# A planned kernel of attention and gated FFN layers: another task order, other planned landing times, fewer zero-tile matmuls at the start

## The chip, the cores and the metric

The kernel runs on one core of one Trainium2 chip. Its time is the device time of one execution in microseconds (us); the median of several runs is compared. A separate profiled execution gives the trace and the profile page.

## What is computed

Four layers follow each other on x (2048 positions of 512 values): recurrent attention, FFN, attention, FFN, the same weights for both pairs. Each adds its result to its input and works on the layer norm of its input.

```python
# attention, 32 heads of 128; 64 segments of 32 positions, with 8 memory rows
for s in range(n_seg):
    h = jnp.concatenate([mem, xs], axis=1)            # 8 + 32 rows
    q, k, v = h @ Wq, h @ Wk, h @ Wv                  # per head
    p = softmax(where(mask, q k^T * scale, -1e9))
    o = (p v) @ Wo
    mem = o[:, :M]; outs.append(o[:, M:])
# FFN: (sigmoid(x @ w_gate) * (x @ w_up)) @ w_down,   512 -> 1792 -> 512
```

The memory makes segment s + 1 wait for segment s, so attention is a chain of 64 steps. Everything is in bf16 with sums in f32.

## The kernel before

**Tiling and stages.** Both attention layers run in one loop of 70 steps (`emit_step`): step t works on segment t of the first layer and segment t - 6 of the second, side by side as 80 columns. In steps 0 to 5 only the first layer has a segment, in steps 64 to 69 only the second: these are the thin steps, with 40 columns. A step takes the heads in six groups. For each group: projections q and k (line 892), a copy out of PSUM on ScalarE (ACT), scores (906), softmax on VectorE (DVE) with the exponential on ACT (920 to 937), transposes of the probabilities (949), a copy that spreads them (`spread`, from line 954), their product with the values (975), a copy, and the product with Wo (993). The end of a step copies the new memory rows into the next step's input `hT` (1006, 1011) and the output rows into `oxT`.

Values come in another way. `v_pass` and `v_half` (695, 732) project whole blocks of positions ahead of time and write them through DMAs to a scratch in DRAM (`scr`); each step reads its slices back into `vsb` (line 861, issued on SyncE, SP). Rows that depend on the memory are projected inside the step, as a strip of 32 columns for all heads (`strips`, 817), and go from `sst` to `vsb` by DMA (line 872, SP). A block of 128 positions (4 steps) that is finished goes through the FFN (`ffn`: transposes 1063, gate and up 1095, down 1119); its weights don't stay in SBUF, so that each of the blocks loads them again by transfers of 256 KB that GpSimd (POOL) issues (1087, 1088, 1113). At the start SP issues all attention weights (`load_weights`, 591), about 16 MB, in a fixed order of arrival, while TensorE (PE) works on values of the first blocks.

**What sets the order.** Nothing is issued where the code stands. Every operation is added to a list of 13,280 tasks (`Planner.add`, 214) with its engines, a planned duration, a latency `lat` until others may use its result, the keys that it reads and writes, and bytes for a DMA. `plan` (251) unpacks `SEQUENCE`, a compressed list that gives each task a rank, and `forward` (272) plays the program through in planned time: whenever an engine is free, it takes the ready task with the lowest rank that its buffers allow. For the kernel before, the ranks in `SEQUENCE` are the order in which the tasks start in that plan. The resulting order is the program: each engine executes its tasks in it, and waits on semaphores where data aren't there yet. So the planned times don't reach the chip; the order does, and so do three things that are drawn from the planned times:

- which of ACT and DVE takes a copy that either could do;
- the pace of the FFN weight loads: each waits on the chip for the PE task that ended just before its planned start (`add_manual_dep`, line 1240), so that POOL, which executes in order, is held by PE;
- zero-tile matmuls: where the plan leaves PE idle for over 250 ns, `warm` (415) puts matmuls of an all-zero tile `hot` ahead of the next task, in pieces of 128 columns, four to an instruction (line 1218). They write to the bank that the next task overwrites.

For transfers the plan keeps a bus time (`bus`, 372) for all DMAs together; a DMA is done at the later of the bus and of the end of its issue plus `lat`. `lat` is 4300 ns for a slice from the scratch (863) and 3200 for a strip (874). SP may have eight transfers under way in the plan (378 to 380).

Of the kernel before, what the change touches and what calls it, by code (L numbers as in the profile page):

```python
# [20 lines left out]
P = 128  # L21
MEM = 8
SEG = 32
L = MEM + SEG
LW = 2 * L
XS = 24
# [27 lines left out]
;Ag)rXk7pcfB%7A@!gH@5PER9zwFwU*Txh6(FIfkX|(7J?i&Gymhh!kX3<9*It9&+^ANuZ3nQF%vjb@k;)ADNDw~7A&yK6rftjYT<(0_Cu$F5_QL}_k&+#M$g4fMAuI3%VR%9II^4edG>hLecVFKKZ  # L54
fiq<zaDy4oUFv58J8W8}M`2{oi5UUb^!f*Ro0Ll?vc4MO@r^c`&wF^g&x{e8(wi=&1jnm{X}@GBNB?B98ftnN@q;Urg_TN7gRljNIZ1xL04!;{jd2yH$?cL&EwR4Y4Tqu8pK|P3tu<gW{h$`ab{UE_
fqK5_Bs&J*b^6-QBtiB1Rm-Zu8Nlc!2f&|gEyzQ&Zou|%s7^3{5zh9KTUR}tya8Oc6!P`{0)Vq8I;Cl`Bjt~AjrB%)CqD@z82Z2w;QrC0`{pXpx_R2Wh&&#2H3QIv3WnP|a@1!GQgacw;pKW^M`R|!
Nk+QQ;DjyYF5GF7!M*<sd8cVD>2uHyj70Z$6aD8lSDtqSMB#M+!9iZef2n{|jXj7clA2G^EzqM!g-lB)@}v+s<dLTg#Kii~);*dJP_OtPjOrD`dCRS`B*?af^G#|5&z)YMf)|%^UO;YbIwUZ94H|;|
&I8kZBVH%Vr|M`z4VQLMuW2mhCo%WGrCP@C3|aBQ!Z@sF?{dn1nHiX-Hcv2SE;6gPREA8v1gxUN5fjwov7s7E=){nUleMkl)rSwf-#NWnt+iLb)vYQSg8NO|ck6a&f5J`jCYy?w$`JBYrP7VoA#kkX
>yw8_VzTSGOpj8yq?_x;;hBH;rz~q4SdF9ZBg{rG@)htW>FtF!fG!q1a8hR)S^e6}q?Lzs^}+^#ob7fH!>Fyt6Ec%(XxD2g=*h~t0x*|HYIgpYBcJ&io_?o{l)`4GU_@%j@)8o~)(WjyR`I-_DVdEX
qpsq`mM61>+(8TaM-5>9Drz=jnb)-=yYKy|4I>K@zHNw@rcCC|=f*ye&WaMflMV5|xPNyTb*H)NgH9?jw1M*`|Aqy&^a*rUk;3mH)kGJznF1RvY3@t@=2^xaH0-f1Ty6gB5>G7cN@NTPLrchUmPhHP  # L60
BPzZ2ia}YU1q5^?Zh`JV^|-uLP^j5y#P_ZT06?ozV2jLQSp96AT@omT@9`T$m-yy@g4kD5^7&#?)KvIhz5<IDDn_B}S$w_%O54$*Uf&%*f!G9A0k)w2S80jRm_OzzD}%&|JCO=Jux2;jsV1&&*ocDe
vv19OW<}n=z=BXtevuQth?wJcFw3v~A;KU0Fj8U7v;-ubd1)6$LvOp^(EF2YN4lWzA>9UsIioM@psu~u&Horxi#{K)nGF~9<5jCnBT^6l!UsB(k4o)!8A~I>f8#r%yu%<R0mYyTfZ<)Sni2UT(vn0#
tm2cI5k@+Ojklj8V{nBRX$UB+gfBzr^hrH>$u5kX5;NqVjvk?&E^!9Un709~&!yGdZ`zS12GJ~~o>$PW0_Q(~(ech%@Dd4F?a@?s&4w?B3X^B#o>$WuxPHlU8E1h;6sRCPM;Cb&M89tcFI3Fc7SaL-
@ko8IZK`J@W2GEGmX}g(7vDTBKpV{0l0Fa*zKW5nQtSNYScG9m-W4oihEpRM9oZhx$s8@o43g~=;)6hTN^z^Shvggyiw$J(S&trHsZko5QCciufS!$?n=$+iEW_#~(`j}&V4WCWgYlK!d#Qs8!?9zj
+bqOxo_kt*eZ7rE@04&B0z8Nz9i<d40QttTz6^4LDi~8yhg8P4NzvULMSQJ-$b!TRs-7IAd_l8GT;#XHgZcX$-$b)HgDh{d9p!Ey5NK#kZ(Nzsu&svhey17&ct5)NozyL<4jW>hTpOmDH`UV?uNeKn
ulL27>(f<<fI2lD7P@{ZxKK5izxo4o_!^ec%pEaQr`~plAyRxTVWrISSzr8X5TfH(1GV1AzqFJC@ZL5V(+q2z_(&=mUZDhaes!D&m_4JvmfF?Tb1D<p2^ZH$QTP$`?ht%YJSK>L&CcqNEJ<!Kr{4oz
vj+K3Emf<Ch%)`ULp{|Z!2<pl7r@(XMSkbViiH_g;!i$l%ewSb&20V3maX%pZQ9=^qZ9wc+A{sGfKnIIgZi9N`Aj$1&p0a=tUVPau*9x6O+3z+=cQwW#v2L`O$oZv0t|=^q0+3wovlZqw;CjluSfY1
7;)b2dM;AEItw!IJo9aZVFG>~c1D!+Q8oJ6gHCVjgh+q=g5RV7n;S4Z{Vb-#GBbB5;S`h<JtFjk*+%dBbL|0-RP<JoBUp$?mRdco7QSmHHji-UX7~{&TCk0xhlix|OcNZzn$a?dwXxy6toswR3nCxg
<$l)jDf(|Z9;2QA2Pa?Sr*59(v?!>Gw*!qSrriD#k;zlQ3O)3BertDQxc3{@%R7C#_YLB_AsNpEq&sbpzKmH~RYP~bk{Zd_?;Wo1EPM{r9g$C}>3;0X_dxzhSf2(<dWtt@E+CAb_+p>QbPZxM{{PS3
*en5KD&!3JofsA3^5fe+Yc=aOqR)fM<|mNjpQ}L_L`b6F5Z9!0Ny_KiYa1f=>UfHv5NT}Dt#)}&@tB}*TmVzJN!1wQ308W#%Ewt9=zute@fBG_bJI~rE8@x(8H9zT)JiPkVik)hOISJpJ`Z|aqfuxS  # L70
9MY^{ThVokOpd=UmpouWZAyJ+>Q&s<TSe0J7BeE=BIr=gLszKqR~2v6Y6>hu2k+cm^UC_1#1b|?t!P7;XyfV~lp@ZnPb$}EWnWzg)_Pm2Q2jbtP7fuO#3di=k)6Dpo<n|F!K`{GgUY<TL&xEiPlsLE
&`&N90i`ZrB`F!^X2xQ#Z*X7g10f8gpm<n@MdGTPU@}*SmWq{(s7(9g_Cv(?{N1{2oaF^jfe$o_VK4qMF^xSK*{cee3e$;(u_$eW`lc&g&EI&y4i*uW%6zw-NX1hb(pOJBbt)zq^a*_i4QZU3OsA`a
ogk8T2n3iX4#2Ol?c4h;A1AqM9wA^Jr*lL?l6X!W4a}idB0|TS{P^F0xoo=H?n}?x#S)J57?AP`%qwl>;dln_?FWE@z$Yf>Vqz`|dwyR1uaTh&cJ&l`kd!X_?-X)Uh(;|b$81Dn>eA?1v=O~yq6@bR
lvtg%>-}E)I4o%t7|qUp0K%C@$IO_3Q8c<f2sy?3NQKPEsTbru3QRD|F$a4d@f{&HJW`|O6+dZE$zQ(5B{Er!7rj;f4B;-AE4MX{;f6HfmZJze6(XM=l9u^A_U!OD95{V?ww{=>wQP72Z~s4Qm*vR?
e*y&gf*;_)**=M^LbI7dC46mRe<kfr+>_l^QZ>lm(OXgC(MLi@qI+N!-8i=oU4&L8DE2q;wf%=IK%<}jzPwj}l6xHHB!-gZcv^HoZ{V!;w_?ExVSCPsDrsA{#Sb51#5b-20&?c^99>Nt=R8W4MSi*l
MCgAULe{=wE<IiLPE}6f&Z9CBTjxxm#$_7R6;Z-ebVg&LO>WXD!Pep6L3A0rMfMW?E%7v;VO`&f|Ap|wZ??;v^Q~wr_4FD&tZm<<vV<O6&>j+yJH$*U-MCo}`YUh|$58?UEU%S|;`YMe5WJlSWE_kL
E)LRM0MQ6r<a(5C^kO>B<W_mrR)FViX&=9@G;RSwumdZ&Qt1(0oIO6ak`3nRTF(wTL^pIe!t#dYVm=<rx<3Qr+huU{k!&q2AKPMS@{}fFPJPOl#O~xT)AjxxLZv|mhvohJ9z}-?!-FGN&=ldq)4r!D
*cp!V%Xw+RfahwLc)Ig{IHF)!SEG<NE#(9Yjhv#WJHTKEisY~5+qr=eRZhP)FaoF64N_9o35pnE(v8PoEVgW0r7x!jM^tenC7jjy!)MB3AcYWC48j5cMuv^}G6mD{UWyge2qtcY@;VQVZW$|axO~Oh
vJ(=-Q@Ew*P=dF|XXgO7`vJ<K48cKaSn5!FbYSw;t|wilbDVKhl?<VuNKghUS_lENW9>r$n!HW<BYwx!DFqn}AM7hQA@+s#m*u9N`b@Ma9m(V@dcecx`>pXpHMrdvT!$c6$7K*gPb#>jO6SUnwQF@S
>&t@I)gR?aZ}gYOy@|#4pu_GanAT5qv_jCS5Bv&znUe*1UBapE&|l`w?O1MdgnZ0R>Mw-E2=S@|2~OEKN1d=5kb0C<kwu$H!>xGujj568I8SGM7M8A~PmPpMktJ_zpry#uUGFxUxwuGjCr~0sf2+7g  # L80
1QQD+ok!zeEc-N#r4j85HjD_IIP7)bE0pBeVVwgpGLUF`aXcEYnas+nct*2CTatDY-UO860yp_D;wWRpnHqVob|AJG7Eu_;>7MspwFG-#th34g)A=(1$WWqkU;dyO*fYj89O$tHXy+9?G6n&!nE-bT
uHD2FL;P#J3)5yM(sJ4mXzUH7K%MW7ut6#aKE_VEm8Zy-<yJf7`JD;Ds5Y`Z;5r^JhiwaiY`Yzu+r<wjQ5Jo3qztp-Yaeftih>wiGv?Z>PImvDU$@!v+b{k6>d0r$Nyk>FDKbk@R8n3?EwnO2Jg_HM
^&{BYQ8~-q2UvBMkkT}=lF||tq88|}HA%Z!Mt#`v=86No_G8L~#*ll=e=mHZvdY}~2W}KZX>Q6&iLKNDoZhI7TM(m#F!*Py7hpHcsLyRcn)4c;_seEgk97w&NXraXv<}|Yrx`T)jmEs3KDJqcrl)v+
a`E{XIOU{=9wyfA_Qe6Fg7PICy+z0rWItXRiR_fcrE1b+YtfpKgby_i#DiZ#q>GE6gKJTEca-j*m_AZaS4r+{5`fIsD&Eka>#T$1h%?;0L<5{vRMqk<8KPEk@Hw2d(cY(lH4`Vc4`a4Z=uhAXua01S
d}N%2@j4-Sn=puE>7zRCBiN}PtDL0phD3sq=I<r8HJ|%r%nhYL7_BikjSVR7+}$I#^phFzOtMlRr9wvktyrcN>^S>5uX~y;KOZ)07B|Qpvfzi}nE<fV`fY&4nmh5Vo=gj<YM<Et2XL=k(Gfy+aAziY
!^T6yS=iPENu&kYb=FMz$XP>`DbpK9ox{*OWEvuP-dmBN%G*ZNlp2hSa77%g8H}Q_vPe%^C_Wp@)l$iHJrqj#=?~-%OjTBz7-kBg`I(xH^>eR@G<Em|wx>|WJt-xLE^W6up^P9~Kzun|byk~JEL#qF
UT%u3pg>u~N>iFXr84s{rky2t>t)1^hbyS|duHgv<R>(*@EcY|68IFb_x<JivX6sMv3lk=G4)l-D|&A(+awSm>pxhC=g<Ailb*)61+`*VtE_9f)yaAZnZx0`&xUz9Bi)0ndpC81IL=Fj>o}=}Ch^mD
a{YD<DQ#UfTxfqfn^-c6BC>YaC?R{qp)yf?p^3FV`^;lp-G8kVmKY3DqUL^S7g8+yJY4Vqq+(;q2YardKTJIIfSm;hAPuL(^{=YS2(t@2CS#O|s>c+=cuo2pLjY8Q$x#DV6Zej6Z6+s2Jao_#6eB^N
7a5P*6g-Zs{MHJT@<NVSs+drmT7C3uX>~(ur1;DdnN#UDYL?v7!!Fre<D_&r)ysX~u$jJpBXkHfi3^CbRQiN2#eVj4*Y&1Y9&Yd62}WPCU&?}1jk)^<;Xj%lk#*xH0J&?acOayDsi(r9Pg2arChoLZ
-c0{UkOgOWe7F;kG@*`6JA3Tn`bJM{0HY}ewITRwN+$1#PQS@f-e0GvY)0$_E>?k<uwxEv0N7%EmpAT;Pguj6d{Vby55>>*K-;Iy`XUw~a}xZd?9AV_f!CW0v1lx`Y@Mez3s_!eUd;`Q1*q_s7(F>=  # L90
4|BDtOk7rIPYp}7tPpCvbDyozSV)N#SL-t8I#V*{;CN%gQSVpsRe{_W<u{-?#aIGWPKK%H>**?-Ee>E?+#s+xtjt>}|33G7$N>I7i12j!u*RF%AAMnT$i@ZE-;Dgde8ZKEW37GCDnvi=le%JSa+G{n
+&Iei>EHmn=Fsxv|3C+uBlYDwTeYMZ&|8yf!>xC<lEgQzP+}DO)!F0Rf-DyHJ&<4G8eX2f+_P;6p&iv_V7UBs;C9F-9w+M|V%Dl{fMndP&kvo}d~iFsz7en-le9_u7*050e=zT3TWENVzx4zpe*EaN
E_R$wJ-6^dPSSK@HOiCva7<DlXkg9$A4q~qoev;f>xEG5`j|;}P6atT6JKHMeOBIUD!T7j@4=|Nf2Mg|DNFxWR&Hobs33JvVoFWbB(+u~7S$IxLqhyuGE&<vvl{CyO&z1oqHfh|2xyX5WdT^mjU{tL
qaiR6CykR9^~7dzlRAX3MnyC%)N&8XzzBT>bv5sR!f20Ha(j*RX9WbB&PIxchc5h=Fmjcqzgq1c{LF1WAx56-)nRxBt(DTxU^e<pf5p<J$)x~lc3BEtc>5LooO%n>XFGs~e{wNRGFTg$-_-?oHq5=9
w4PjSRCtdm*_=uiYlvVz!YpcU&k&0W4`R>fm7lQteSFF!M_52KaD|hF4CV}>6@KAW_}6k%yr)uH5D+@!u!nR>=?c#?EH^}0gd<j=cI~S7NNJIjZ-;~~8~e*@$)xkTbtoPX8<ePoaKkwZfMKsxKmi0a
GuEMV*kIW9?cN!r2{Z}sRkM}Hp5K)F0tm@-G^~vb{o~t{NOIx4)$8Ga?v>%CZ73bbqe-h(VGLXgCktybTz0o?*E>l{R4ioO9icVr#Jc5)aU&C~A(1}LPak#aaOk$ttY*Q>Q>`CmI4~tQH4Rm@q>AcG
?R9df05%CgU-Pl14SM+nGMMPk&7`&ID>$|s48-otrEtg9kZZs)L+Zk9Nq1c>2IhbA`rKc1L|lOdv395d@BqQ!ZW)c&jT3=)jt-4AomSOAN>}-+7UgX$PQR8kPkU=(C_~M3H8RWgDI*wT6%5ZSNsgs^
@`+tryad9d!c$`q7#<gIBN`WEv|-=;q=6=-NNKI5N(Z+cjzi^+wN~=rb_XnLICCEjg{eVEW=&t+zXa@WrA38tA1)DC&=s`b`b6z{%beoMIYj(s$g%D*K;Hz;p&*5f%6hl7ZLwiUm$bqc=)TbL>Z(9z
# [55 lines left out]
class Task:  # L154
    __slots__ = ("eng", "dur", "lat", "fn", "deps", "succ", "tail", "boost", "ndep", "ready", "start", "idx", "on", "fresh", "acq", "rel", "durs", "tick", "prev", "land", "adj", "banks", "rate", "nb", "after")

    def __init__(self, eng, dur, lat, fn, boost):
# [6 lines left out]
        self.adj = {}  # L164
        self.banks = ()
        self.rate = 0.95
        self.nb = 0
        self.after = None


# [19 lines left out]
class Planner:  # L190
# [9 lines left out]
    SPAN, COLD, WARM0 = 3413.0, 8000.0, 1200.0  # L200
# [1097 lines left out]
```

## Time and profile before

| | |
|---|---|
| median of 3 runs | 1785.14 us (1785.05 to 1786.47) |
| span of the profiled execution | 1781.3 us |
| instructions | 91,977 |
| matmuls recorded | 39,873, of them 109 of the zero tile |
| DMA traffic | 270.66 MB, mean 152 GB/s |
| granted TensorE clock | 1.000 |

The span runs from the first to the last instruction of one profiled execution; the runs of the table's first row are timed apart from it and 3.8 us longer. In the profile PE stands for matmuls and PEld for weight loads, which overlap them; ends of matmuls are modelled, and a few of the 512-column records are missing. SPq and POOLq are the queues that issue DMAs. A row of a timeline gives start, duration, engine, line, operation, output and input names, how many instructions were merged, and in brackets the idle time of the engine before it and what ended it. `L1232` and `L1234` are the helper lines through which all copies go.

### The profile page before, as it was taken

The numbers are of one execution on the slowest core, as the hardware profiler recorded it, in microseconds if no ns is written. First come the engines' busy times: TensorE is split into PE (matmuls) and PEld (weight loads), VectorE is DVE, ScalarE is ACT, GpSimd is POOL, SyncE is SP. The second block draws the span as 40 slices with busy tenths as digits, with TensorE's granted clock in tenths as the row PEclk, the third lists the DMA queues.
The fourth block names the chain that finished last, engine by engine and source line by source line (L and its number), as shares of the span: only waits on it lengthen the run. The fifth ranks groups of instructions, "written<-read, shape, count | busy, mean of one in ns | idle before, by whom it ended". The sixth has DMA issues, their size and how long they took to land.

```text
span 1781.3 us, 91977 instructions
## 1 busy us (share of the span) xinstructions
PE 1754.0 (98%) x39873; PEld 1517.1 (85%) x40083; DVE 1144.1 (64%) x3931; ACT 1167.8 (66%) x2973; POOL 573.8 (32%) x828
## 2 busy tenths in 40 slices
PE   9999999999999999999999999999999999999998
PEld 4688888888888898989898898988888888989886
DVE  4376666776577666756666676657656665666675
ACT  6676666666666666666766666666666766667564
POOL 5314031513233242323324241333324232333332
PEclk9999999999999999999999999999999999999999
DMA  9825254635555464445546453555555454555543
GB/s 342 265 74 165 59 155 121 195 105 158 146 162 153 133 174 136 139 137 165 160 130 198 135 161 106 154 160 167 156 148 172 111 145 140 158 156 139 165 143 94
DMA packets 131943, 270.66 MB, mean 152 GB/s; under 512 B 30394, under 2 KB 65090, under 8 KB 131538
## 3 DMA queue, kind: packets, MB, share of 16 engines
q0 software_dynamic: 56240, 181.91, 34.7%
q1 hardware_dynamic: 75298, 82.86, 16.3%
q8 instruction: 314, 5.14, 1.3%
q14 instruction: 91, 0.75, 0.1%
HBM read 220.41 MB, written 25.69 MB: 138 GB/s over the span
## 4 chain that ended last, share of the span: by engine, by line
PE 91%; DVE 5%; ACT 2%; issue 1%; DMA 1%; SPq 1%; POOL 0%; ACTq 0%; DVEq 0%; POOLq 0%
PE bank L892 31%; PE bank L993 17%; PE bank L1095 11%; PE bank L695 8%; PE bank L817 7%; PE bank L975 4%; PE bank L906 4%; PE bank L1119 4%; PE bank L949 2%; DVE st L920 1%; PE bank L1218 1%; PE bank L664 1%; DVE small L925 1%; DVE small L932 1%; DVE st L927 1%
## 5 line engine op out<-in xcount | busy, mean ns | idle before, releaser
L892 PE MATMUL bank<-hT,wq_sb 128*128 128x80 bf16 (+1 forms) x8960 | 622.6, 198 | 1.3 <-issue 0.6
L892 PE MATMUL bank<-hT,wk_sb 128*128 128x80 bf16 (+1 forms) x8960 | 622.5, 198 | 0.6 <-issue 0.6
L1232 ACT CAST qku<-bank 128x480 bf16<-128x480 f32 (+3 forms) x770 | 388.3, 512 | 222.5 <-PE bank L892 142.0
L892 PEld LDWEIGHTS <-wq_sb 128*128 128x128 bf16 x8960 | 454.1, 99 | 35.0 <-issue 25.1
L892 PEld LDWEIGHTS <-wk_sb 128*128 128x128 bf16 x8960 | 450.8, 99 | 0.8 <-issue 0.7
L920 DVE TENSOR_TENSOR st<-bank,cst 40x240 f32<-40x240 f32 (+3 forms) x768 | 277.7, 367 | 200.9 <-PE bank L906 194.2
L993 PE MATMUL bank<-otsb,wo_sb 128*128 128x80 bf16 (+1 forms) x8960 | 362.8, 198 | 1.9 <-ACT otsb L1232 0.2
L993 PEld LDWEIGHTS <-wo_sb 128*128 128x128 bf16 x8960 | 336.7, 99 | 16.3 <-issue 1.9
L1087 POOL DMA_DIRECT2D wg<-in_B_w_gate_dram x217 | 164.0, 756 | 299.1 <-PE bank L1095 109.8
L1232 ACT CAST otsb<-bank 128x480 bf16<-128x480 f32 (+3 forms) x420 | 199.8, 482 | 59.6 <-PE bank L975 47.6
L1088 POOL DMA_DIRECT2D wu<-in_B_w_up_dram x217 | 163.9, 756 | 197.3 <-PE bank L1095 89.3
L1113 POOL DMA_DIRECT2D wd<-in_B_w_down_dram x217 | 153.8, 709 | 213.4 <-PE bank L906 74.5
L930 ACT ACTIVATE st<-st 80x240 f32<-80x240 f32 (+3 forms) x420 | 159.5, 381 | 39.9 <-DVE st L927 37.1
L654 POOL TENSOR_TENSOR small<-small,cst 128x1 f32<-128x1 f32 (+1 forms) x80 | 44.8, 562 | 413.7 <-DVE small L653 410.2
L1095 PE MATMUL bank<-xnT,wg 128*128 128x128 bf16 (+2 forms) x1784 | 172.0, 219 | 0.8
L1095 PE MATMUL bank<-xnT,wu 128*128 128x128 bf16 (+2 forms) x1784 | 171.2, 219 | 0.0
L906 PE MATMUL bank<-qku 128*128 128x80 bf16 (+1 forms) x2240 | 161.0, 198 | 1.5 <-ACT qku L1232 0.2
L932 DVE TENSOR_REDUCE small<-st 80x6 f32<-80x240 f32 (+3 forms) x420 | 150.6, 360 | 16.3 <-ACT st L930 14.0
L937 DVE TENSOR_TENSOR pb<-st,small 80x240 bf16<-80x240 f32 (+3 forms) x420 | 153.6, 368 | 4.2
L927 DVE TENSOR_TENSOR st<-st,small 80x240 f32<-80x240 f32 (+3 forms) x420 | 154.1, 368 | 3.1
L925 DVE TENSOR_REDUCE small<-st 80x6 f32<-80x240 f32 (+3 forms) x420 | 151.4, 362 | 4.6
L975 PE MATMUL bank<-ptsb,vsb 104*128 104x80 bf16 x2048 | 140.2, 199 | 3.0 <-DMA vsb<-sst 1.5
(102 smaller groups left out, 2345.2 us busy)
## 6 DMA issues: line engine op xcount, KB each, us to landing
wg<-in_B_w_gate_dram POOLq DMA_DIRECT2D x220, 256.0 KB, 4.3
wu<-in_B_w_up_dram POOLq DMA_DIRECT2D x220, 256.0 KB, 4.3
wd<-in_B_w_down_dram POOLq DMA_DIRECT2D x220, 256.0 KB, 4.3
vsb<-scr SPq DMA_DIRECT2D x460, 48.0 KB
vsb<-sst SPq DMA_DIRECT2D x464, 32.0 KB
scr<-vst SPq DMA_DIRECT2D x112, 96.0 KB
wv_sb<-in_A_Wv_dram SPq DMA_DIRECT2D x8, 512.0 KB
wo_sb<-in_A_Wo_dram SPq DMA_DIRECT2D x10, 384.0 KB
```

The source lines that it names most:

```text
L892: nc.tensor.matmul(o_ap, lhsT=W[:, c, h * P:(h + 1) * P], rhs=mv(c), start=(c == 0), stop=(c == DC - 1))
L906: nc.tensor.matmul(s_all(SB)[:, w0 + i, :], lhsT=fview(qku[:, i, 0, 0:1], [(1, P)]), rhs=qku[:, i, 1, 0:ncol], start=True, stop=True)
L920: pl.add("DVE", dve_ns(n, True), lambda gsz=gsz, hs=hs, st=st, SB=SB, pj_=pj_, npj_=npj_, mk=mk, idx=idx: nc.vector.tensor_tensor(out=st[p ...
L925: pl.add("DVE", dve_ns(n), lambda hs=hs, st=st, mx=mx: nc.vector.tensor_reduce(out=mx[pr, hs], in_=st[pr, hs], axis=AX.X, op=ALU.max), r=s ...
L927: pl.add("DVE", dve_ns(n), lambda gsz=gsz, hs=hs, st=st, mx=mx: nc.vector.tensor_tensor(out=st[pr, hs], in0=st[pr, hs], in1=mx[pr, hs].uns ...
L932: pl.add("DVE", dve_ns(n), lambda hs=hs, st=st, sm=sm: nc.vector.tensor_reduce(out=sm[pr, hs], in_=st[pr, hs], axis=AX.X, op=ALU.add), r=s ...
L975: nc.tensor.matmul(fview(OB[:, o:o + 1], [(ncol, 2), (1, L)]), lhsT=self.vsb[halves[u // 8]][0:64 + L, j, (u % 8) * P:(u % 8 + 1) * P], rh ...
L993: nc.tensor.matmul(WB[:, c * ncol:(c + 1) * ncol], lhsT=self.wo[:, h, c * P:(c + 1) * P], rhs=otsb[:, hl, 0:ncol], start=(h == 0 and c == ...
L1087: pl.add("POOL", 760, lambda wg=wg, fs=fs: nc.gpsimd.dma_start(out=wg[:], in_=self.wgv[:, :, fs]), r=[("wo", self.H - 1)], w=[gk] + bt, la ...
L1088: pl.add("POOL", 760, lambda wu=wu, fs=fs: nc.gpsimd.dma_start(out=wu[:], in_=self.wuv[:, :, fs]), r=[("wo", self.H - 1)], w=[uk] + bt, la ...
L1095: nc.tensor.matmul(gu[:, 2 * i + k, 0:n], lhsT=W[:, c, i * P:(i + 1) * P], rhs=xnT[:, c, rw], start=(c == 0), stop=(c == DC - 1))
L1232: nc.scalar.copy(out=dst, in_=src)
```

## The change

The list of tasks stays the same. Five things change:

1. `SEQUENCE` is another list of ranks (78 lines of text, not shown).
2. A DMA task can have a factor `slow`. The plan keeps a second bus time, `wbus`, for the FFN weight loads on POOL alone, and adds to the latency of a task with `slow` that factor times the backlog of these loads, up to `BACK` = 2300 ns. Slices from the scratch get 2425 ns and factor 1, strips 2800 ns and factor 0.6.
3. The slices of step 0 also wait for the load of Wo that holds the last head.
4. `warm` counts zero tiles otherwise at the beginning: the time up to `COLD` (now 4400 ns) counts at half the rate, and the first gap starts at 1000 ns in the place of 1200.
5. The plan's duration of the second `spread` copy is 52 ns more if DVE does it.

```diff
-    SPAN, COLD, WARM0 = 3413.0, 8000.0, 1200.0
+    SPAN, COLD, WARM0, BACK = 3413.0, 4400.0, 1000.0, 2300.0
...
-        bus = 0.0
+        bus = wbus = 0.0
...
-                    done = max(bus + self.TAIL, end + tk.lat)
+                    done = max(bus + self.TAIL, end + tk.lat + tk.slow * min(max(wbus - now, 0.0), self.BACK))
+                    if e == "POOL" and tk.nb >= self.BIG:
+                        wbus = max(wbus, now + self.LEAD[e]) + tk.nb / self.BUS
...
-                cold = tk.start < self.COLD
+                cold = end < self.COLD
...
-                    n = int((gap - 120.0) * (1.2 if cold else 2.4)) // P
+                    n = int((gap - 120.0) * 2.4 - (min(tk.start, self.COLD) - end) * 1.2 * cold) // P
...
-                        r=[("vd", j, b, q, kk) for q in range(lo // 8, (lo + nx) // 8) for kk in (h0 // 4, h0 // 4 + 1)], w=[("vx", j, vh, i)], lat=4300.0, nb=nx * 2048)
+                        r=[("vd", j, b, q, kk) for q in range(lo // 8, (lo + nx) // 8) for kk in (h0 // 4, h0 // 4 + 1)] + ([("wo", self.H - 1)] if t == 0 else []), w=[("vx", j, vh, i)], lat=2425.0, nb=nx * 2048, slow=1.0)
...
-                        r=[(sb, 0), (sb, 1)], w=[(name, j, vh, i)], lat=3200.0, use=[sb], nb=nr * 2048)
+                        r=[(sb, 0), (sb, 1)], w=[(name, j, vh, i)], lat=2800.0, use=[sb], nb=nr * 2048, slow=0.6)
...
                 d["ACT"] += 93.0 * i
+                d["DVE"] += 52.0 * i
```

## The prediction

> **What bounds the kernel now.** I read the page first, then who TensorE (PE) waits for, then five stages, then the first 90 us engine by engine.
>
> ```profile
> span 1781.3 us, 91977 instructions
> ...
> PE 1754.0 (98%) x39873; PEld 1517.1 (85%) x40083; DVE 1144.1 (64%) x3931; ACT 1167.8 (66%) x2973; POOL 573.8 (32%) x828
> ...
> PE 91%; DVE 5%; ACT 2%; issue 1%; DMA 1%; SPq 1%; POOL 0%; ACTq 0%; DVEq 0%; POOLq 0%
> ```
>
> PE is the bound, and the change leaves its real work alone. How much of 1781.3 us is work? Busy time can't say, since the ends of matmuls are modelled; the starts can. In stretches without a wait they follow each other every 25 ns (40 columns), 36 (80), 56 (128) and 216 (512), and a strip task of 32 matmuls takes 1.85 us. Times the counts by shape (for 512 columns the counts of the code, since some records are missing) that is 1719 us of work. The other 62 us are all that an order can save. Placed by the same starts: 12.0 before the first real matmul, 2.8 more up to 50 us, 2.1 from 50 to 100, 13.3 from 100 to 250, 15.0 from 250 to 1650, 11.1 from there to the last matmul, 3.7 behind it, and 2 of rounding. Zero-tile matmuls (line 1218) lie inside these sums. By stages:
>
> ```profile
> 100.00:250.00 150.00, 146.19 (x3774) 125.40 (x3788) 97.16 (x344) 97.83 (x281) 34.69 (x48) 1.00 0.39 109
> 250.00:1650.00 1400.00, 1384.90 (x31325) 1229.04 (x31496) 915.57 (x3134) 929.62 (x2300) 456.37 (x631) 1.00 0.52 149
> 1650.00:1781.00 131.00, 125.16 (x3467) 105.65 (x3474) 85.19 (x296) 75.16 (x251) 42.66 (x59) 1.00 0.46 133
> ```
>
> Columns: stretch, length, busy time of PE, weight loads, DVE, ACT, POOL, clock, DMA share, GB/s. By the starts the long middle loses 1%, the stretch from 100 to 250, where mostly one layer runs, 9%. PE's waits on transfers are small (in total, times, longest):
>
> ```profile
> PE bank L1063 <- ACT oxT L1232: 3.5, 8, 0.5
> PE bank L975 <- DMA vsb<-sst: 1.5, 2, 1.0
> ```
>
> **Step 1, fewer zero tiles.** The start of PE, then the first normalised block that it transposes:
>
> ```profile
> 1.00 11.14 PE L1218 MATMUL bank<-hot 128*128 128x512 bf16 x43 [1.00 <-DVE small L564]
> 11.98 0.39 PE L664 MATMUL bank<-cst,xn 128*128 128x128 bf16 x4
> 12.20 1.30 PE L1218 MATMUL bank<-hot 128*128 128x512 bf16 x6
> 13.34 0.39 PE L664 MATMUL bank<-cst,xn 128*128 128x128 bf16 x4
> ```
>
> ```profile
> 9.31 0.40 DVE L655 TENSOR_SCALAR xn<-xs,small 128x512 bf16<-128x512 bf16 x1
> ```
>
> xn is ready at 9.71, yet PE transposes it at 11.98: for 2.27 us nothing but the 43 zero matmuls stands before it. They are 172 tiles of 128 columns, and the old formula, (gap - 120) * 2.4 / 128, gives 172 for a gap of some 9.3 us, so the planner had the first transposes at 1.2 + 9.3 = 10.5 us. It overlooked the slow beginning: by their starts the first 8 matmuls take 0.424 us each (1.00 to 4.39), the rest 0.216. The new formula takes it into account: gap 9.5 from WARM0 = 1.0, (9500 - 120) * 2.4 - (4400 - 1000) * 1.2 = 18,432, over 128: 144 tiles, 36 matmuls. They would end at 1.00 + 8 * 0.424 + 28 * 0.216 = 10.44 instead of 11.96: **1.51 us earlier**, still behind xn at 9.71. If the new order plans that first transpose elsewhere, the formula follows, so the saving lies between 0 and 2.27; I take 1.5. The next fill (21 tiles, 1.13 us) is past both COLD values, and I leave it.
>
> The Trainium skill speaks against taking zero tiles away: "TensorE: Matmul & The Clock Gate", Part 1 (What's actually happening), says that the array runs at 1.2 GHz until it has been busy for a window of about 3.4 us, and again after an idle one. The row agrees on the length (3.39 us at 0.424). By the rule too few tiles would cost a second slow beginning, about 3.4 us at half speed, so 1.7 us (an estimate from that page), which would eat the gain. By the rows there is no idle window: 36 matmuls reach 10.44, xn waits since 9.71. I take the rows, and 1.7 us as the bad end.
>
> **Step 2, the order at the beginning.** Unpacked, each sequence is a rank for each of the same 13,280 tasks. Before, the ranks are the order of planned starts. After, they are priorities (a score of step 2 ranks first, which cannot run first), so the order made of them isn't to be read off. But where they moved can be seen: of the PE tasks that started in the first 300 us 186 of 661 moved by over 20 places among PE's tasks against their stage's median, from 400 us on 5 or fewer in each 100 us. So steps 250 to 1781 us stay nearly as they were, with 26 us of loss that I leave in place (at +-1). What can be saved lies in the 15.4 us between 50 and 250, and one stall there shows of what kind it is:
>
> ```profile
> 171.29 0.76 POOL L1087 DMA_DIRECT2D wg<-in_B_w_gate_dram  x1 [1.96 <-PE bank L993]
> 172.04 0.70 POOL L1113 DMA_DIRECT2D wd<-in_B_w_down_dram  x1
> 172.76 0.57 POOL L654 TENSOR_TENSOR small<-small,cst 128x1 f32<-128x1 f32 x1
> 173.37 0.41 DVE L655 TENSOR_SCALAR xn<-xs,small 128x512 bf16<-128x512 bf16 x1 [1.71 <-POOL small L654]
> 173.84 0.40 PE L664 MATMUL bank<-cst,xn 128*128 128x128 bf16 x4 [0.92 <-DVE xn L655]
> ```
>
> A power of 0.57 us stands behind two paced weight loads on POOL, and PE goes without work for about 1.3 us, one zero tile included. Another order may avoid such cases; it can also make new ones. Steps 1 to 3 of the recurrence take 16.0, 16.7 and 16.9 us each (first projections at 85.5, 101.5, 118.2, 135.1) for some 14 us of PE work, so much of the loss is the chain of a step itself. Bounds: -6 (40% of 15.4) and +4 (three more stalls like this one). I take -2.5, two such stalls.
>
> **Step 3, latencies and the new wait.** The plan's landing times become 2.4 us plus the backlog of FFN loads, up to 4.7, for slices from scratch (before 4.3), and 2.8 up to 4.2 for strips (before 3.2). Counting a slice's landing as the last increment of its semaphore, the trace has a median of 1.8 us with no FFN load under way and 3.4 to 3.6 with two to four: the new shape is the nearer one. No instruction is added; what it can save is what PE lost to such landings, 1.5 us above, 0 at the other end. I take -0.5. The DVE price of the spread (+52 ns) only shifts copies between ACT and DVE, both a third idle: 0.
>
> New on the chip is one wait: step 0's four slice loads stand behind the Wo load of the last head. On SP, queued behind them, are the rest of Wo and x:
>
> ```profile
> 57.78 2.05 SPq L861 DMA_DIRECT2D vsb<-scr  x3
> 59.87 0.37 SPq L794 DMA_DIRECT2D xs<-in_A_x_dram  x1
> 60.39 0.28 SPq L861 DMA_DIRECT2D vsb<-scr  x1
> 63.84 0.36 SPq L591 DMA_DIRECT2D wo_sb<-in_A_Wo_dram  x1
> ```
>
> These four were issued at 57.8 to 60.7; between 56.6 and 63.8 no weight was asked for. Last-head Wo was asked for at 69.3 and landed at about 73.5. Moved behind that, four issues of 0.4 and 2.4 us land at 77.5; PE uses them first at 76.9. Cover gone: about 0.6 us late. Against that the weights can be asked for earlier in the freed 6 us. The two cancel; bounds -1 and, if Wo is late, +5 (the rival below).
>
> **Sum.** -1.5 - 2.5 - 0.5 = -4.5: 1776.8 against the span of 1781.3. The median is 3.84 above that span, which I take as what lies around it: 1785.14 - 4.5 = **1780.6 us**.
>
> **Rivals.**
> *Absorbed (no change), 0.30.* Up to 80 us the transfers run at a share of about 1.0, and the last Wo part lands near 80, just before step 0 uses it (82.5). A PE that is 1.5 us ahead then waits 1.5 us for Wo, or has 1.5 us fewer value products to fill the thin steps. For it: the thin steps are latency bound. Against: PE loses only 2.1 us from 50 to 100, since other work is at hand. With the ends of steps 2 and 3 at nothing: 1785; with a little of each, 1784.
> *Slower, 0.20.* The wait on last-head Wo decides when the chain of layer 1 begins. If that load, moved in the new order, lands after 74 us, each us of delay moves step 0's attention. At the place of the last Wo load before (asked 72.8, landed about 78.2) the slices land at 78.2 + 1.6 + 2.4 = 82.2, 5.3 us after 76.9, with the thin steps behind and no slack in them; less the 1.5 of step 1: 1785.1 + 3.8 = 1789.
> *Faster, 0.50*, as summed; its own range is 1776 to 1781.5.
>
> **How the numbers follow.** A measurement of this kernel can tell about 0.2% (3.6 us) from no change, so faster means under 1781.6. I give 0.50 to that, 0.30 to the absorbed case and its neighbours, 0.20 to slower. Range: 1775.5 (step 2 at its end of -6, the last us of step 3 and the middle's -1) to 1788.5 (the slower rival nearly whole); about 1 in 10 is left out on either side.
>
> **What would show it.** Step 1: some 36 zero matmuls first, transposes of xn at about 10.4. Step 2: less loss between 50 and 250, step 6 (first projections at 177.5 before) starting 3 to 5 us earlier. Step 3: slices of step 0 issued after 69 us, PE's first use of them not after 78. The middle unchanged to 1 us. Wrong would be: first transposes early but step 1 still at 85.5 (absorbed), or PE waiting for slices near 77 to 82 (slower), or new stalls of the middle, where ranks moved by a few places.

## The result and the profile after

The changed kernel takes 1789.91 us in the median of 10 runs (1786.43 to 1793.49). The kernel before, on the same chip, takes 1783.74 (10 runs, 1781.8 to 1786.47). The ratio is 1.0033, with a 95% interval of 1.0024 to 1.0042: 5.9 us slower by these medians. The prediction was 1780.6 us, and it gave slower a chance of 0.20. The profiled execution has a span of 1787.7 us, 6.4 longer than that of before. Four of the ten runs show a granted clock of 0.999 or 0.998; the other six, at 1.000, have a median of 1789.4 us, so a lower clock is not the main cause of the 5.9 us.

First the page of after (span; busy time; the chain by engines; the group of value products, with mean ns of one and the idle time ahead of it):

```profile
span 1787.7 us, 92147 instructions
...
PE 1764.9 (99%) x40078; PEld 1517.9 (85%) x40078; DVE 1159.2 (65%) x3973; ACT 1160.6 (65%) x2931; POOL 575.1 (32%) x830
...
PE 92%; DMA 2%; SPq 2%; DVE 2%; ACT 1%; issue 1%; POOL 0%; DVEq 0%; POOLq 0%; ACTq 0%
...
L979 PE MATMUL bank<-ptsb,vsb 104*128 104x80 bf16 x2048 | 137.5, 200 | 7.5 <-DMA vsb<-scr 2.9
```

and the last of these lines as it was before:

```profile
L975 PE MATMUL bank<-ptsb,vsb 104*128 104x80 bf16 x2048 | 140.2, 199 | 3.0 <-DMA vsb<-sst 1.5
```

PE's share rises from 98 to 99%, but the busy sums of the two can't be compared: the trace of before lacks 210 of the 512-column records, that of after none. What counts is the chain: SP's queue and DMA hold 4% of it, where they held 2% before. The value product (line 979, before 975) now waits 7.5 us, before it was 3.0. The same three stages as before:

```profile
100.00:250.00 150.00, 147.10 (x3800) 125.86 (x3798) 97.64 (x352) 98.99 (x278) 32.11 (x45) 1.00 0.36 101
250.00:1650.00 1400.00, 1390.65 (x31424) 1226.52 (x31422) 926.72 (x3151) 921.17 (x2267) 455.31 (x630) 1.00 0.52 149
1650.00:1788.00 138.00, 130.25 (x3593) 110.04 (x3589) 89.62 (x316) 77.04 (x251) 44.92 (x62) 1.00 0.46 132
```

The clock is 1.00 in each stage of this execution. Who PE waits for, after:

```profile
PE bank L1067 <- ACT oxT L1236: 3.2, 7, 0.5
PE bank L979 <- DMA vsb<-scr: 2.9, 2, 1.5
PE bank L979 <- DMA vsb<-sst: 2.7, 6, 0.8
...
PE bank L979 <- DVE ptsb L1238: 1.4, 1, 1.4
```

Two waits on slices (`vsb<-scr`) of up to 1.5 us are new, strips (`vsb<-sst`) cost 2.7 where they cost 1.5, and one wait of 1.4 on DVE is new.

**Where the time went.** A marker that can be followed is the start of a step's first projections (line 892 before, 895 after). In us, from the two timelines of PE:

| step | 1 | 6 | 12 | 18 | 24 | 30 | 36 | 48 | 60 | 69 |
|---|---|---|---|---|---|---|---|---|---|---|
| before | 85.49 | 177.53 | 327.59 | 482.76 | 634.71 | 787.70 | 937.97 | 1246.67 | 1550.81 | 1747.37 |
| after | 87.49 | 178.45 | 327.11 | 485.09 | 635.77 | 791.00 | 944.85 | 1252.19 | 1555.52 | 1754.39 |
| difference | +2.0 | +0.9 | -0.5 | +2.3 | +1.1 | +3.3 | +6.9 | +5.5 | +4.7 | +7.0 |

At step 12 the new order is level with the old one. Most of the loss comes between steps 24 and 36, at 635 to 945 us, in the middle that the prediction had left alone; another 2.3 us come between steps 60 and 69. (The markers tell when a step starts, not how well PE is filled up to there, since an order can also move FFN work and value blocks past a marker.) The new order's own plan, which the kernel works out while it is built, ends at 1768.85 us, that of the old one at 1769.07: the plan promises 0.2 us. The chip departs from it by some 16 us after and some 9 before, so the question is what the plan doesn't see.

Two stalls of that stretch, in the timeline of PE after:

```profile
705.18 0.20 PE L979 MATMUL bank<-ptsb,vsb 104*128 104x80 bf16 x1
706.75 0.57 PE L979 MATMUL bank<-ptsb,vsb 104*128 104x80 bf16 x11 [1.37 <-DMA vsb<-scr]
...
909.79 0.20 PE L979 MATMUL bank<-ptsb,vsb 104*128 104x80 bf16 x1
911.50 0.34 PE L979 MATMUL bank<-ptsb,vsb 104*128 104x80 bf16 x5 [1.50 <-DMA vsb<-scr]
```

and what SP's queue issued ahead of them:

```profile
700.22 1.54 SPq L1232 DMA_DIRECT2D scr<-vst  x2
701.80 3.02 SPq L864 DMA_DIRECT2D vsb<-scr  x5
...
907.84 1.08 SPq L1232 DMA_DIRECT2D scr<-vst  x1
909.01 0.75 SPq L864 DMA_DIRECT2D vsb<-scr  x2
```

PE has done one product and cannot go on: its slice is still under way. The third of the five slices at 701.80 was issued at 703.70 and its last increment came at 706.70; PE goes on at 706.75. The second slice at 909.01 was issued at 909.40 and landed at 911.25; PE goes on at 911.50. Landing took 2.7 and 1.5 us from the end of the issue, nothing unusual: over the whole trace slices land after a median of 2.9 us with 9 in 10 under 4.3, and in before after 2.8 and under 4.1. They were issued late. From 896.91 to 909.40 SP issued 20 transfers one behind the other; in that time it fell from 10.05 to 12.62 us behind the plan (PE's product at 909.79 was 10.15 us behind it), because an issue took 0.3 to 1.1 us where the plan has 0.375 (slice), 0.40 or 0.65 (scratch write) and 0.60 (strip). And the new plan leaves less room for that. In its own times, 36 of the 1024 slice and strip loads are used less than 3.5 us after their issue ends; in the old plan 13 are (below 4.5 us: 89 and 61). A slice planned to land 2.4 us after its issue, instead of 4.3, may be issued nearer to its use, and the planner made use of it.

### The profile page after: what moved, and what is told of

Its sections match the earlier page's. It is cut to its first block, busy times and chain, and to the rows that moved or that the text cites. A ratio compares the mean times of both kernels' runs of the same rounds, so it can differ in the third digit from the quotient of the medians.

```text
span 1787.7 us, 92147 instructions
## 1 busy us (share of the span) xinstructions
PE 1764.9 (99%) x40078; PEld 1517.9 (85%) x40078; DVE 1159.2 (65%) x3973; ACT 1160.6 (65%) x2931; POOL 575.1 (32%) x830
## 4 chain that ended last, share of the span: by engine, by line
PE 92%; DMA 2%; SPq 2%; DVE 2%; ACT 1%; issue 1%; POOL 0%; DVEq 0%; POOLq 0%; ACTq 0%
PE bank L895 31%; PE bank L997 17%; PE bank L1099 11%; PE bank L698 8%; PE bank L820 7%; PE bank L1123 5%; PE bank L979 4%; PE bank L909 4%; PE bank L952 2%; SPq L875 1%; DMA vsb<-sst 1%; PE bank L1222 1%; PE bank L667 1%; DMA xs<-in_A_x_dram 1%; PE bank L1067 1%
## 5 line engine op out<-in xcount | busy, mean ns | idle before, releaser
L909 PE MATMUL bank<-qku 128*128 128x80 bf16 (+1 forms) x2240 | 165.2, 198 | 0.5 <-ACT qku L1236 0.3
```

The lines of the kernel that those rows point to most:

```text
L909: nc.tensor.matmul(s_all(SB)[:, w0 + i, :], lhsT=fview(qku[:, i, 0, 0:1], [(1, P)]), rhs=qku[:, i, 1, 0:ncol], start=True, stop=True)
```

## The experiments

The theories, as the expectations name them. **S**: PE waits for slices and strips that come late. **O**: the new order is worse by itself, whatever lands when. **B**: the transfers themselves became slower. **X**: the x load and the layer norm on DVE at 81 us hold the end of step 0. In the last four runs: **W**, what remains is the wait for the last Wo parts and x near 80 us; **G**, it is waits for FFN weights; **N**, neither. All ratios are against the kernel before on the same chip, with 95% intervals.

### The zero tiles alone

Before with the new count of zero tiles (first diff), after with the old one (the second).

```diff
-    SPAN, COLD, WARM0 = 3413.0, 8000.0, 1200.0
+    SPAN, COLD, WARM0 = 3413.0, 4400.0, 1000.0
...
-                cold = tk.start < self.COLD
+                cold = end < self.COLD
...
-                    n = int((gap - 120.0) * (1.2 if cold else 2.4)) // P
+                    n = int((gap - 120.0) * 2.4 - (min(tk.start, self.COLD) - end) * 1.2 * cold) // P
```

```diff
-    SPAN, COLD, WARM0, BACK = 3413.0, 4400.0, 1000.0, 2300.0
+    SPAN, COLD, WARM0, BACK = 3413.0, 8000.0, 1200.0, 2300.0
...
-                cold = end < self.COLD
+                cold = tk.start < self.COLD
...
-                    n = int((gap - 120.0) * 2.4 - (min(tk.start, self.COLD) - end) * 1.2 * cold) // P
+                    n = int((gap - 120.0) * (1.2 if cold else 2.4)) // P
```

> The order of before with the new count of zero tiles alone. Both theories: the first transposes start 1.0 to 1.5 us earlier. If the start is carried through: 1782.3 (-1.4). If it is absorbed where the last Wo and x loads land at about 80 us: 1783.7, step 1's first projections at 85.5 as before.

> The order of after with the old count of zero tiles. Carried through: 1 to 1.5 us slower than after (1791). Absorbed at 80 us: the same as after, 1789.9 +- 0.5, with the wait of 1.4 us at 82 us gone or smaller.

Measured: before with the new count 1783.6 us, 1.0001 (0.9992 to 1.0009); after with the old count 1794.59, 1.0064 (1.0052 to 1.0077). So the smaller count alone gives nothing that can be measured, as "absorbed" had it, though a gain of 1.4 us stands just at the edge of the interval, and in the profiled execution the first transposes came only 0.27 us earlier, not 1.0 to 1.5 (step 1 of the prediction, below, has the reason). The other result meets neither expectation: seven zero matmuls more at the beginning, in the same order, cost another 5 us. They are not lost there: against after, step 1 of the profiled execution starts 0.9 us later, step 36 1.1 and step 69 4.1. The value product of that kernel, what its idle time waited for in total us and times:

```profile
its engine sat idle before it (us, times) until:
  issue: 11.3, 18
  DMA vsb<-scr: 5.2, 4
  DMA vsb<-sst: 4.6, 6
```

Those of after are 5.6 (14 times), 4.4 (3) and 4.3 (8), those of before 4.0 (13) for issue and 2.1 (3) for strips. From 600 to 1000 us PE loses 9.0 us there, against 7.4 after and 3.2 before (by the starts of its matmuls, as the prediction counted). In these three executions, the slower one is, the more PE waits for values. Why a shift of some 1 us at the beginning turns more slices late isn't shown.

### PE doesn't wait for slices

In both orders the value product reads a part of Wo in the place of the slices; every load is still issued.

```diff
-                                         lhsT=self.vsb[halves[u // 8]][0:64 + L, j, (u % 8) * P:(u % 8 + 1) * P],
+                                         lhsT=self.wo[0:64 + L, u, 0:P],
```

> The order of before, but the value product reads a part of Wo as its weights and not the value slices, so PE never waits for a slice load (all loads are still issued; the output is not the attention's). Theory S (late slices: the changed order puts value slices too close to their use, and PE waits for them): before loses only some 3 us to slices, so 1780 to 1782 us. Theory O (the order itself: copies, softmax and weights of the new order cost the time, slices play no part): the same 1780 to 1783; this run is the base for the next.

> The same edit in the order of after (the output is not the attention's). Theory S: the 8 to 9 us that PE waits for slices in its trace go, so 1780 to 1782 us, within 2 us of the same edit before. Theory O: it stays 5 to 7 us above the same edit before, so 1786 to 1788.

Measured: before 1783.89, 1.0005 (0.9997 to 1.0013); after 1786.72, 1.0016 (1.0009 to 1.0024). The distance between the orders, 2.8 us, lies between what S (within 2) and O (5 to 7) expected. It falls from 0.0033 to 0.0011, so about two thirds of the loss are waits for slices and strips (S); the fall of 0.0022 has an error of about 0.0014. In the trace PE's idle time at the value product falls to 1.5 us for issue (7 times) and 1.2 for DVE (once), and from 600 to 1000 us its loss falls from 7.4 to 3.1 us; but this execution, at 1781.89 us, is the fastest of the 21, and can't stand for the median. Something like 2 us may remain; one blemish is that the edit lets step 0 read Wo, which this order loads late.

### SP issues less

The scratch writes of the later blocks are left out (so values of those segments are those of the first blocks), and slices read blocks that are there. The slices keep their place in the order.

```diff
-... lambda vs=vs, d=d, c0=c0, n=n: ("dma", d, vs[c0:c0 + BLK * n, 0:512 * w]), ...
+... lambda vs=vs, d=d, c0=c0, n=n, b=b, j=j: ("dma", d, vs[c0:c0 + BLK * n, 0:512 * w]) if boot or b <= 2 * (j == 0) else None, ...
...
-... r0=s * XS + lo, nx=nx: nc.sync.dma_start(
+... r0=(s if j == 0 and s < 8 else s % BLK + 8 * (j == 0)) * XS + lo, nx=nx: nc.sync.dma_start(
```

> The order of before, with nearly all later writes of value blocks to the scratch left out (SP has some 200 issues fewer) and the slices read from the blocks written first (the values are not the attention's). Theory S (slices land late because SP's long bursts of issues fall behind the plan): before has slack for it, so no more than 1 us less: 1782 to 1783.5. Theory B (slices land late because the shared transfers are slower than planned, SP has no part in it): the same.

> The same edit in the order of after. Theory S: SP's bursts are shorter, slices are issued when planned, and the 3 us that reading no slices gave come here too: 1786 to 1787.5. Theory B: it stays at 1789 to 1790, slice waits in the trace as in after (8 to 9 us).

Measured: before 1782.99, 0.9994 (0.9986 to 1.0002); after 1784.89, 1.0011 (1.0005 to 1.0018). The distance falls to 0.0017 (error about 0.0010), though PE's products still read the slices. Waits of PE for `vsb` in this kernel:

```profile
PE bank L979 <- DMA vsb<-sst: 1.5, 3, 0.6
```

The waits on slices are gone and those on strips fall from 2.7 to 1.5. This execution (1785.56 us) is a typical one, and in it PE loses 3.8 us from 600 to 1000 us where after loses 7.4; step 36 starts 1.4 us behind that of g_before, where after stood 6.9 behind before. About half of the loss thus hangs on the scratch writes that stand ahead of the slices in SP's queue. The writes also carried 14 of 82 MB of that hardware queue's bytes; so less traffic may have helped too, but the landing times, nearly equal in before and after, speak against B as the cause of the difference.

### The end of step 0

The stall at 82 us, in the timeline of after (PE's product waits for a copy on DVE, which is behind a layer norm's statistics, which wait for x):

```profile
81.01 0.69 DVE L654 BATCH_NORM_STATS2 small<-xs 128x6 f32<-128x512 bf16 x1 [2.04 <-DMA xs<-in_A_x_dram]
81.62 0.22 DVE L1230 TENSOR_SCALAR ptsb<-bank,small 104x40 bf16<-104x40 bf16 x1
...
81.97 0.20 PE L979 MATMUL bank<-ptsb,vsb 104*128 104x80 bf16 x1 [1.40 <-DVE ptsb L1238]
```

In m_after_earlyx the x loads of blocks 2 and 3 go ahead of waiting Wo loads on SP; in n_after_earlyx_noslice the values edit is added to it.

```diff
+def early_x(T, order):
+    sp = [tk for tk in order if tk.on == "SP"]
+    for i in range(len(sp)):
+        k = i
+        while k and sp[k].early and not sp[k - 1].early and sp[k - 1].start >= max(sp[k].ready, 69500.0):
+            p, q = sp[k - 1], sp[k]
+            p.start, q.start = q.start, p.start
+            sp[k - 1], sp[k] = q, p
+            k -= 1
...
+        pl.tasks[-1].early = b in (2, 3)
...
-        order = self.pl.plan()
+        order = early_x(self.pl.tasks, self.pl.plan())
```

> The order of after, but on SP the two loads of x that are issued at 72.8 and 74.5 us go ahead of the last Wo loads (issued at about 70). Theory X (the start's gain is lost at 82 us because DVE, in order, holds a waiting layer-norm statistic of a late x block ahead of the spread copies that PE needs): the wait of 1.4 us at 82 us goes, 1 to 2 us faster than after, 1788 to 1789. Its rival, that Wo itself sets the time there: the wait moves to the products with Wo, time as after, 1789.5 to 1790.5.

> Both edits in the order of after: early x, and the value product reads a part of Wo and not the slices (the output is not the attention's). If slice waits and the wait at 82 us are the whole loss: at or below the same edit in before, 1782 to 1784. If a third cause stays: 1785.5 to 1787, as with the slice edit alone.

Measured: 1790.18, 1.0039 (1.0026 to 1.0053), and 1786.11, 1.0015 (1.0006 to 1.0024). Both stand where they stood without the early x, so X falls. In m_after_earlyx the wait of 1.4 us is gone, as meant, and PE meets the next thing (line 1013 is the product with Wo here; the execution is the fastest of five, 1786.89 us):

```profile
84.50 0.97 PE L1013 MATMUL bank<-otsb,wo_sb 128*128 128x40 bf16 x32 [0.73 <-DMA wo_sb<-in_A_Wo_dram]
```

The last Wo parts are late as well: the new order asks for six of the twelve only from 70.22 us on, the old one for three.

### PE waits for no load

Four runs ask what the 0.0011 are that f_after kept. k_before_noload and k_after_noload add to the values edit that gate and up read Wq and Wk, and down reads Wo, in the place of the FFN weights, which are still loaded at their pace:

```diff
-                    for k, W in ((0, wg), (1, wu)):
+                    for k, W in ((0, self.wq), (1, self.wk)):
...
-... rhs=wd[:, k, :], start=(i == 0), stop=(i == FC - 1))
+... rhs=self.wo[:, i, :], start=(i == 0), stop=(i == FC - 1))
```

w_before_nowo and w_after_nowo have the early x, value products that read Wq, and an output product that reads Wq in step 0:

```diff
-                                         lhsT=self.vsb[halves[u // 8]][0:64 + L, j, (u % 8) * P:(u % 8 + 1) * P],
+                                         lhsT=self.wq[0:64 + L, 0, u * P:(u + 1) * P],
...
-... lhsT=self.wo[:, h, c * P:(c + 1) * P],
+... lhsT=self.wq[:, c, h * P:(h + 1) * P] if t == 0 else self.wo[:, h, c * P:(c + 1) * P],
```

> The kernel before with the values edit of f_before (the value product reads a part of Wo, not the slices) and, further, gate and up read Wq and Wk and down reads Wo in the place of the paced FFN weights; every load is still issued. PE waits for no slice and no FFN weight. All theories: 0.999 to 1.0005 of the kernel before, since its waits for FFN weights are under 1 us in sum.

> The same two edits in the kernel after. f_after alone stood at 1.0016 (the like edit of the kernel before at 1.0005). Theory W (the 2 us that f_after still lacks are the wait for the last Wo parts and x near 80 us): the FFN weights are not in it, 1.0010 to 1.0018. Rival G (they are waits of gate, up and down for weights that the new order asks for too late): 0.9998 to 1.0007. Rival N (neither; the order itself is slower): 1.0010 to 1.0018 as well, told from W by w_after.

> The kernel before with the value product reading a part of Wq in the place of the slices, the output product of step 0 reading Wq in the place of Wo, and the x loads of blocks 2 and 3 put ahead of waiting Wo loads on SP. PE waits in step 0 for no Wo part. All theories: 0.999 to 1.001 of the kernel before; it lost only 1.6 us from 75 to 100 us as it was.

> The same edits in the kernel after (n_after_earlyx_noslice with the output product of step 0 reading Wq). n_after stood at 1.0015. Theory W (the last Wo parts hold step 0 near 80 us and that stays in the end): the loss from 75 to 100 us falls from 3.7 to under 2.0 us and the time to 0.9998 to 1.0006. Rivals G and N: the loss there may fall, but the time stays at 1.0010 to 1.0018, since the chain takes it back later or what is left lies elsewhere.

Measured: k_before 1781.68 and k_after 1781.96, both 0.9991 (0.9984 to 0.9997). w_before 1784.61, 1.0007 (0.9999 to 1.0015), w_after 1783.77, 1.0001 (0.9993 to 1.0009). In k_after (the fastest execution of 21, 1779.00 us) the list of PE's waits has no transfer among its first three rows:

```profile
PE bank L1067 <- ACT oxT L1236: 3.2, 7, 0.5
PE bank L979 <- DVE ptsb L1238: 1.6, 1, 1.6
PE bank L997 <- ACT otsb L1236: 1.1, 3, 0.6
```

Where PE doesn't wait for values and FFN weights, the two orders take the same time, within 0.0009. So O falls as an account of the 5.9 us, and N with it. Between W and G these ratios don't decide. Either edit takes the rest away, and each distance (0.0000 and -0.0006) has an error of about 0.001, as large as the rest itself. The traces don't decide either: PE waits 2.0 us for FFN weights in f_after, but still 1.6 in w_after, and the loss from 75 to 100 us, which W wanted under 2.0 us, stayed at 4.0 there, because something else was late:

```profile
85.09 0.61 PE L713 MATMUL bank<-wv_sb,xvf 128*128 128x512 bf16 x2 [1.08 <-issue]
```

**The clock of the timed runs.** One more thing differs between the orders, and no theory above names it. Each timed run has its own granted clock. It lies below 1.000 (mostly at 0.999; 0.001 of 1785 us is 1.8 us) in these numbers of runs:

| kernel | runs below 1.000, of all |
|---|---|
| before, timed beside these experiments | 5 of 139 |
| h_before, f_before, g_before, k_before, w_before | 0 of 13, 0 of 13, 0 of 13, 1 of 21, 1 of 13 |
| after, h_after, f_after, g_after | 4 of 10, 2 of 5, 13 of 21, 5 of 21 |
| m_after, n_after, k_after, w_after | 4 of 5, 7 of 13, 13 of 21, 0 of 13 |

In f_after the eight runs at 1.000 have a median of 1783.6 us, as f_before has (1783.9); the thirteen below have 1787.7. So what f_after kept goes with the lower clock. In k_after the eight runs at 1.000 have 1780.2, 1.5 us less than those of k_before: where PE neither waits for these loads nor runs at a lower clock, the new order may even be a little better. w_after, which differs from n_after in that step 0 doesn't read Wo at all, is the only one of the new order without such runs. That speaks for W, the late Wo parts, as the place, but it rests on counts alone: every kept trace is of a run at 1.000, so where the clock fell, and whether a stall brought it down or the other way round, isn't shown.

## Why the prediction was wrong

**What bounds the kernel: right.** PE's work is the same 1719 us in both by the starts; its loss up to the last matmul grew from 58.8 to 65.5 us, 6.7 more, against 6.4 in the spans. The base was a little high: the 3.84 us that it took for what lies around the span are 1.7 to 1.9 in the runs on record, and the median of before over ten runs is 1783.74, 1.4 under that of the first three. Also the lower end of its range, summed as it says, is 1775.1 and not 1775.5. Neither matters for the outcome.

**Step 1, fewer zero tiles (-1.5): mis-sized, and absorbed.** The planner put in 146 tiles, 37 matmuls (forecast some 36), and the start of PE in after is this:

```profile
1.00 10.09 PE L1222 MATMUL bank<-hot 128*128 128x512 bf16 x37 [1.00 <-DVE small L567]
10.92 0.39 PE L667 MATMUL bank<-cst,xn 128*128 128x128 bf16 x4
```

The transposes start at 10.92 in the place of 11.98: 1.06 us saved, not 1.5. One matmul more costs 0.2, and the slow beginning was ten matmuls long here, not eight, another 0.4. Its length isn't fixed. In h_before_newfill 36 zero matmuls took longer than the 37 here, and the transposes began at 11.71:

```profile
0.99 10.88 PE L1218 MATMUL bank<-hot 128*128 128x512 bf16 x36 [0.99 <-DVE small L564]
```

The first 14 were slow there; in h_after_oldfill it was 7. So the page's row moves by up to 7 * 0.21 = 1.5 us from one execution to the next, as much as the edit. The Trainium skill has the reason ("TensorE: Matmul & The Clock Gate", Part 1, What's actually happening): the activity window runs freely, so where a kernel's start falls in it is chance; one sentence there puts the spread at +-0.5 us, another says that one kernel showed 6, 11 or 14 slow matmuls. These executions, 7 to 14, or 2.9 to 5.9 us from the first zero matmul on, agree with the second. The second slow beginning that the same page made one fear didn't come in this trace; all of the loss before 14 us fell, from 13.3 to 12.3. The gain was gone by step 1, which started at 87.49 instead of 85.49: the rival "absorbed" had that part right, with its place, near 80 us. That late Wo parts hold PE there shows in m_after_earlyx, which waits 1.2 us for them; after itself waits 1.4 us for DVE, so its cause was right in part at most.

**Step 2, the order at the beginning (-2.5; "steps 250 to 1781 us stay nearly as they were"): this is the step that failed.** It had put the saving between 50 and 250 us, and step 6 was to start 3 to 5 us earlier. It started 0.9 us later, and PE's loss in that stretch rose from 15.4 to 18.5 us, 2.7 of the rise before 100 us. From step 1 to step 12 the markers of the new order do come 2.5 us closer, but PE loses 1.0 us more between them: work was moved behind them, not saved. And the sentence about the middle was wrong. That few ranks moved there by over 20 places said nothing about waits: a slice load needs to move by only two or three places among SP's instructions, at some 0.5 us each, to land a microsecond later. Between 400 and 1000 us PE lost 4.8 us more than before (7.2 to 11.9), and f_after and g_after show that as waits for slices that SP issues late. The prediction had named this sign of being wrong ("new stalls of the middle, where ranks moved by a few places"), but gave it no cost. It should have asked of every load how far its issue stands ahead of its use, not how far tasks moved.

**Step 3, latencies (-0.5, bounds -1.5 and 0): wrong sign.** It took the new planned latency for a better description, which can only save. For the median it is nearer. But the old 4.3 us stood above what 9 slices in 10 need (4.1 us from the end of the issue), and so held a reserve that also covered SP's late issues. A latency nearer to the median lets a load be planned closer to its use, and an issue that runs late then reaches PE. The waits for values (f) are worth about 0.0022, 4 us of the 5.9, within 2.5 us. That the latencies rather than the new ranks by themselves brought the loads nearer to their use is argued from the plan; ranks and latencies were made for each other, and no run here holds one without the other.

**The new wait on the chip (step 0's slices behind the last Wo): there is none.** The key stands in the plan only, since a slice load doesn't touch Wo, and it holds nothing back there: without it the planner's order is the same, task for task, on all five engines. The prediction misread which load it is. The load with the last head (128 KB) is the one that before asks for at 63.84 us; the one at 69.3 brings another head. And the new order asks for it at 38.14 us, long before step 0's four slices, issued at 51.7 to 59.8; they had been forecast after 69. So the rival "slower" was right in the sign and wrong in its mechanism, its place (77 to 82 us) and its point of decision; its 1789 us is near the 1789.91 by accident. The range ended at 1788.5.

**What stays open:** what makes up the last third (0.0011, about 2 us, itself hardly above its error): it goes with the runs at a lower clock, but where the clock falls in them no trace shows; how much of the rest comes from the latencies and how much from the ranks; and why seven zero matmuls more at the start of the new order made it 5 us slower.

## What to carry to other kernels

A planned latency is also the reserve for everything the plan doesn't model. This case suggests putting it at what nearly all transfers need, issue queue included, and not at the median; no run here tested the latency alone. When an order changes, read for each load the distance from its issue to its first use in the new order, since a move of two places in an in-order queue can cost a stall that no count of moved tasks shows. A gain at the start of a chain can be gone where a later transfer sets the time, so follow it to the next marker before it enters the sum. And look at the granted clock of every timed run, not only at that of the one that was profiled.

## What the runs showed of the hardware

- The slow beginning of PE lasted 7, 8, 10 and 14 zero matmuls of 0.42 us in four executions, to 3.9, 4.4, 5.2 and 6.9 us; a single profile can't size an edit of 1 us there.
- SP's cost of an issue isn't a constant: in one burst of 20 transfers it lay between 0.31 and 1.08 us, and a queue that executes in order adds all of it to its last load.
- The granted clock of a timed run was between 0.997 and 1.000: below 1.000 in 13 of 21 runs of f_after, with a median 4.1 us above that of its other eight, and in none of the 13 runs of f_before.
